# The first four down-score matmuls at the head of each score burst

## The chip, the cores and the metric

The kernel runs on one core of a Trainium2 chip. The metric is the device time of one execution in microseconds. Three runs of the kernel before gave 315.98, 316.63 and 320.5 us; the median is 316.63.

## The reference

An attention block with two branches feeds a two-matrix MoE expert. Shapes: batch B = 8, H = 8 heads, S = 576 positions, D = 64. Cut to what is computed:

```python
q_d, k_d, v_d = (mean over 4 neighbouring positions of q, k, v)   # 144 positions
out_up = repeat(sm_attn(q_d, k_d, v_d), 4, axis=2)                # "down" branch
mask = abs(pos[:, None] - pos[None, :]) < 4                       # "local" branch
scores = where(mask, q @ k.T / sqrt(D), -1e9)
out_local = softmax(scores) @ v
x = (out_up + out_local) as [B * S, H * D]                        # 4608 x 512
h = x @ w_in                                                      # 512 x 2048
out = (h * sigmoid(1.702 * h)) @ w_out                            # 2048 x 512
```

## The kernel before

The 4608 tokens go through the MoE in nine groups of 512 (loop `for g in range(n_groups)`). `mm1` multiplies by `w_in` (128x512 matmuls, L682) and applies the activation on ScalarE (L693); `mm2` multiplies by `w_out` (L746). The attention of batch g + 1 is woven into group g. The order on each engine is written by hand: `POS` and `POS_G` name the steps of `mm1` and `mm2` ahead of which a part of the attention is issued. The parts are, for each batch: the first score burst (`s_pe(0)`, four of the eight heads), its exponentials (`s_act(0)`), the second score burst with its exponentials (`s1`), two steps that multiply by v (`av`, L439 and L448), and the transposes (`tr`, L490). Each stands on TensorE as a short burst between long MoE matmuls. Batch 0 has its own functions (`scores`, `scores_d`) in the start-up part and runs before the loop, so `scores_mixed` is called for batches 1 to 7, twice each.

A score burst (`scores_mixed`) has two kinds of matmuls on small tiles of the array, each with a weight load of its own. A local score (`score`, L367) takes 32 rows of the array and 64 columns and streams 60 columns; there are 80, in groups of four over the four 32-row strips. A group of one `x` uses one 64-column half for even strips and the other half for odd ones, the next group the opposite halves. A down-score (`score_d`, L379) has the same tile size, streams 144 columns, and is issued in sets of four, one per strip; there are six sets (three chunks `kc` times two halves `a` of D), 24 matmuls. The locals write two PSUM buffers `sp`, the down-scores a third, `sd`; the three buffers `pa` serve all parts of the attention in turn.

What the burst reads: `kT` and `qT` come from VectorE transposes (L267); `kdT` and `qdT`, the sums over four positions, from GpSimd (`pool_qk`, L297 and L301), in batch 1's second burst from VectorE (L286). Its results are read by ScalarE: `exp_local` (L417) reads the two `sp` buffers, `exp_down` (L423) the `sd` buffer. The second burst of a batch writes the same three buffers, so it waits for these exponentials.

An instruction that waits for one semaphore does so itself. Where a weight load waits for two engines, a separate semaphore instruction stands ahead of it; the trace shows it on the weight loads' sequencer. In the kernel before, the first weight load of L379 in the second burst of batches 2 to 7 waits for ScalarE and GpSimd.

Of the kernel before, what the change touches and what calls it, by code (L numbers as in the profile page):

```python
# [19 lines left out]
def kernel(  # L20
# [51 lines left out]
    def ps_tile(n=None):  # L72
        if n is None:
            n = turn["a"] % 3
            turn["a"] += 1
        return PA[n]
# [286 lines left out]
    def score(b, qd, sp, i, a, par, r, barred=False):  # L363
        rows = slice(32 * r, 32 * r + 32)
        k0 = 114 * i + KSTART[par]
        q0 = 114 * i + QSTART[par]
        nc.tensor.matmul(  # L367
            sp[r // 2][64 * par : 64 * par + 64, r % 2, 60 * i : 60 * i + 60],
            lhsT=kT[b, qd][rows, k0 : k0 + 64, a],
            rhs=qT[b, qd][rows, q0 : q0 + 60, a],  # L370
            start=(a == 0 and not barred),
            stop=(a == 1 or barred),
            tile_position=(32 * r, 64 * par),
            skip_group_check=barred,
        )

    def score_d(b, qd, sd, kc, a, r):
        rows, j = slice(32 * r, 32 * r + 32), r % 2
        nc.tensor.matmul(  # L379
            sd[64 * j : 64 * j + 64, r // 2, SD * kc : SD * kc + SD],  # L380
            lhsT=kdT[qd][rows, 48 * kc : 48 * kc + 64, a],
            rhs=qdT[b, qd][rows, :, a],
            start=(a == 0), stop=(a == 1),
            tile_position=(32 * r, 64 * j),
        )
# [16 lines left out]

    def scores_mixed(b, qd):
        sp, sd = [ps_tile(), ps_tile()], ps_tile()
        for i in range(5):
            for a in range(2):
                if i >= 2:
                    for r in range(4):
                        score_d(b, qd, sd, i - 2, a, r)
                for x in (1, 0):  # L410
                    for r in range(4):
                        score(b, qd, sp, i, a, r % 2 if x == 0 else 1 - r % 2, r)
        return sp, sd
# [230 lines left out]
    def attention(b, slots=None):  # L644
        st = {}

        def s_pe(qd):
            st["s", qd], st["d", qd] = scores_mixed(b, qd)
# [232 lines left out]
    for g in range(n_groups):  # L881
        b = g + 1
# [74 lines left out]
```

## Time and profile before

| what | value |
|---|---|
| median of three runs | 316.63 us |
| profiled execution | 317.56 us |
| its span, first to last instruction | 315.8 us |
| granted TensorE clock | 0.998 |
| matmuls of L367, mean life of one | 1280, 198 ns |
| matmuls of L746 and L682 (into `pm`), mean life | 528 and 512, 380 and 379 ns |
| one mixed score burst, first matmul to next MoE matmul | 0.99 us |

Times are microseconds from the start of the span. In a timeline row the columns are start, length, engine, source line, operation, destination and sources, tile of the array, operand shape and count; several instructions of one kind are merged into one row, and its length runs to the end of the last. PE is TensorE's matmuls, PEld its weight loads. Matmuls overlap: the life of one is longer than the distance to the next. An end of a matmul is modelled, a start is recorded.

### The profile page before, as it was taken

What the parts mean: (1) busy time and instruction counts of PE and PEld (TensorE: products, weight loads), DVE (VectorE), ACT (ScalarE), POOL (GpSimd) and SP (SyncE); (2) the same over time, 40 slices, a digit from 0 to 9 for tenths busy, and PEclk for the clock granted to TensorE, in tenths of its full rate; (3) what the DMA queues carried; (4) which work ended last, traced back from release to release, by engine and by line L of the source; (5) the groups of instructions that cost most, each with busy time, mean ns of one, the idle gap of its engine ahead of it and who ended that gap; (6) DMA issues with size and microseconds to landing.
All of it is one profiled execution on the core that took longest, in us unless ns stands there. A gap on an engine that the chain in (4) does not pass through costs nothing.

```text
span 315.8 us, 10270 instructions
## 1 busy us (share of the span) xinstructions
PE 307.7 (97%) x4543; PEld 154.3 (49%) x4543; DVE 123.5 (39%) x247; ACT 190.2 (60%) x348; POOL 138.8 (44%) x170
## 2 busy tenths in 40 slices
PE   7989999999999999999999999999999999999995
PEld 3455455445544455455544554455445544444444
DVE  6763824720673057604760377027801640000000
ACT  5445882767657685668566856584767576316611
POOL 8863782179339920794079505960393000000000
PEclk9999999999999999999999999999999999999999
DMA  7999999999959913995299519971920110020011
GB/s 119 122 187 210 187 86 205 190 196 261 181 162 224 202 47 98 188 204 113 87 203 206 112 56 206 208 136 39 173 46 11 58 71 2 15 85 33 2 66 66
DMA packets 64075, 39.97 MB, mean 127 GB/s; under 512 B 44064, under 2 KB 55456, under 8 KB 64032
## 3 DMA queue, kind: packets, MB, share of 16 engines
q1 hardware_dynamic: 44496, 24.32, 36.0%
q0 software_dynamic: 19392, 14.95, 33.5%
q8 instruction: 35, 0.57, 0.8%
q14 instruction: 8, 0.07, 0.1%
q10 hardware_dynamic: 144, 0.07, 0.1%
HBM read 44.83 MB, written 9.44 MB: 172 GB/s over the span
## 4 chain that ended last, share of the span: by engine, by line
PE 91%; DMA 4%; ACT 1%; POOL 1%; issue 1%; DVE 0%; POOLq 0%; DVEq 0%; ACTq 0%
PE pm L746 36%; PE pm L682 35%; PE pa L682 4%; PE pa L367 2%; PE pa L439 2%; DMA qb<-in_q_dram 2%; PE pa L490 2%; PE pa L379 2%; PE pa L746 2%; PE pa L448 2%; DMA vb<-in_v_dram 1%; PE pm L761 1%; ACT od L610 1%; PE pm L640 0%; POOL vb L221 0%
## 5 line engine op out<-in xcount | busy, mean ns | idle before, releaser
L746 PE MATMUL pm<-w_out_bf,gT 128*128 128x512 bf16 x528 | 120.3, 380 | 0.0
L682 PE MATMUL pm<-xT,w_in_bf 128*128 128x512 bf16 x512 | 119.2, 379 | 0.5 <-ACT xT L603 0.3
L693 ACT ACTIVATE gT<-pm 128x512 bf16<-128x512 f32 x128 | 76.3, 598 | 43.7 <-PE pm L682 43.7
L682 PEld LDWEIGHTS <-w_in_bf 128*128 128x128 bf16 x576 | 55.7, 98 | 66.9 <-issue 1.1
L746 PEld LDWEIGHTS <-gT 128*128 128x128 bf16 x560 | 52.3, 98 | 60.7 <-issue 0.5
L431 DVE TENSOR_TENSOR es<-es,mask 128x600 bf16<-128x600 bf16 x28 | 19.0, 694 | 97.0 <-ACT es L417 96.3
L297 POOL TENSOR_TENSOR pq<-kT 128x576 f32<-128x576 bf16 x13 | 15.1, 1165 | 60.8 <-DVE kT L267 60.8
L731 ACT ACTIVATE osb<-pm 128x512 f32<-128x512 f32 (+2 forms) x35 | 20.4, 587 | 25.8 <-PE pm L746 23.0
L476 DVE TENSOR_TENSOR y<-pa,rc 128x896 bf16<-128x896 f32 x28 | 30.6, 1092 | 1.0
L480 ACT COPY y<-y 64x64 bf16<-64x64 bf16 x28 | 6.7, 241 | 31.3 <-DVE y L476 31.3
L417 ACT ACTIVATE es<-pa 128x600 bf16<-128x600 f32 x32 | 19.7, 668 | 8.7 <-PE pa L367 8.6
L313 POOL TENSOR_TENSOR v<-v 112x512 f32<-112x512 f32 x18 | 23.0, 1279 | 0.0
L307 POOL CAST vb<-vf 128x2560 bf16<-128x2560 f32 x6 | 13.9, 2318 | 19.8 <-DMA out_dram<-osb 6.3
L267 DVE STREAM_TRANSPOSE kT<-kb 128x576 f32<-128x576 f32 x16 | 19.9, 1246 | 5.8 <-DMA kb<-in_k_dram 5.6
L733 DVE TENSOR_SCALAR osb<-pm 128x128 f32<-128x128 f32 x1 | 0.3, 292 | 55.2 <-ACT osb L731 55.2
L632 DVE TENSOR_TENSOR xT<-pa,od 128x456 bf16<-128x456 bf16 (+2 forms) x84 | 16.6, 255 | 12.3 <-ACT od L610 12.1
L267 DVE STREAM_TRANSPOSE qT<-qb 128x576 f32<-128x576 f32 x16 | 19.9, 1243 | 0.8 <-DMA qb<-in_q_dram 0.4
L682 PE MATMUL pa<-xT,w_in_bf 128*128 128x512 bf16 x64 | 20.0, 379 | 0.0
L610 ACT COPY od<-pa 128x256 bf16<-128x256 bf16 (+1 forms) x56 | 18.3, 410 | 1.1 <-PE pa L490 0.4
L367 PEld LDWEIGHTS <-kT 32*64 32x64 bf16 x1280 | 14.2, 104 | 6.9 <-issue 4.1
L221 POOL DMA_DIRECT2D vb<-in_v_dram x20 | 13.7, 703 | 8.6 <-DMA w_in_bf<-in_moe_w_in_dram 3.6
L367 PE MATMUL pa<-qT,kT 32*64 32x60 bf16 x1280 | 16.5, 198 | 0.5 <-DVE qT L267 0.5
(90 smaller groups left out, 275.9 us busy)
## 6 DMA issues: line engine op xcount, KB each, us to landing
out_dram<-osb SPq DMA_DIRECT2D x35, 256.0 KB, 2.4
vf<-in_v_dram SPq DMA_DIRECT2D x60, 128.0 KB, 6.8
v<-in_v_dram SPq DMA_DIRECT2D x36, 192.0 KB, 5.4
kb<-in_k_dram POOLq DMA_DIRECT2D x16, 288.0 KB, 7.7
qb<-in_q_dram POOLq DMA_DIRECT2D x16, 288.0 KB, 8.9
w_in_bf<-in_moe_w_in_dram POOLq DMA_DIRECT2D x4, 512.0 KB, 9.2
w_out_bf<-in_moe_w_out_dram POOLq DMA_DIRECT2D x4, 512.0 KB, 12.5
vb<-in_v_dram POOLq DMA_DIRECT2D x20, 64.0 KB, 5.9
```

The source lines that it names most:

```text
L267: nc.vector.transpose(out=t32.rearrange("p (i c) -> p c i", c=18), in_=store[b, qd].bitcast(FP32).rearrange("p (c d) -> p c d", c=18),)
L313: eng.tensor_tensor(out=t1[0:112], in0=x[:, :, 0:2, :], in1=x[:, :, 2:4, :], op=ALU.add)
L367: nc.tensor.matmul(sp[r // 2][64 * par : 64 * par + 64, r % 2, 60 * i : 60 * i + 60], lhsT=kT[b, qd][rows, k0 : k0 + 64, a], rhs=qT[b, qd] ...
L417: nc.scalar.activation(out=es[2 * qd + u][:, :, 0:300], in_=sp[u][:, :, 0:300], func=AF.Exp, scale=inv_sqrt_d,)
L431: nc.vector.tensor_tensor(out=ev, in0=ev, in1=mask, op=ALU.mult)
L476: nc.vector.tensor_tensor(out=y.rearrange("p (x c) d -> p x c d", x=2), in0=ov[:, :, :, 0:D], in1=rc.to_broadcast([128, 2, 7, D]), op=ALU. ...
L610: nc.scalar.copy(out=od[:, 4 * t0 : 4 * (t0 + n)].rearrange("p (t f) -> p t f", f=4), in_=x[:, xx, c0 : c0 + n, None].to_broadcast([128, n ...
L632: nc.vector.tensor_tensor(out=sub(xT[hp], t0 + at, *dims), in0=sub(x, col, *from_x), in1=sub(od, at, *dims), op=ALU.add,)
L682: nc.tensor.matmul(acc, lhsT=w_in_bf[:, dmc, ffc * 128 : (ffc + 1) * 128], rhs=xT[dmc][:, g * TG : g * TG + TG], start=(dmc == 0), stop=(d ...
L693: nc.scalar.activation(out=gT[:, ffc, :], in_=acc, func=AF.Silu, scale=GELU_SCALE)
L731: eng.activation(out=osb, in_=ap, func=AF.Copy, scale=1.0 / GELU_SCALE)
L746: nc.tensor.matmul(ops[t], lhsT=gT[:, ffc, t * 128 : (t + 1) * 128], rhs=w_out_bf[:, ffc, :], start=(ffc == 0), stop=(ffc == n_ffc - 1),)
```

## The change

`scores_mixed` keeps a list of the six sets of down-scores. The first set is issued ahead of all locals. The others follow as before, one set ahead of each group of eight locals from chunk i = 2 on, until the list is empty. So the order in a burst was 32 locals, then six times (4 down-scores, 8 locals); it becomes 4 down-scores, 32 locals, five times (4 down-scores, 8 locals), 8 locals. On the other engines the order of instructions is the same in both kernels.

```diff
     def scores_mixed(b, qd):
         sp, sd = [ps_tile(), ps_tile()], ps_tile()
+        down = [(kc, a) for kc in range(3) for a in range(2)]
+
+        def next_down():
+            kc, a = down.pop(0)
+            for r in range(4):
+                score_d(b, qd, sd, kc, a, r)
+
+        next_down()
         for i in range(5):
             for a in range(2):
-                if i >= 2:
-                    for r in range(4):
-                        score_d(b, qd, sd, i - 2, a, r)
+                if i >= 2 and down:
+                    next_down()
                 for x in (1, 0):
                     for r in range(4):
                         score(b, qd, sp, i, a, r % 2 if x == 0 else 1 - r % 2, r)
```

## The prediction

> **What bounds the kernel.** I read the busy table, the chain of waits, then the timeline of TensorE inside one score burst and around its start. The first two, from the page:
>
> ```profile
> PE 307.7 (97%) x4543; PEld 154.3 (49%) x4543; DVE 123.5 (39%) x247; ACT 190.2 (60%) x348; POOL 138.8 (44%) x170
> ...
> PE 91%; DMA 4%; ACT 1%; POOL 1%; issue 1%; DVE 0%; POOLq 0%; DVEq 0%; ACTq 0%
> ```
>
> TensorE is the bound and has almost no idle time, so whatever a score burst gains or loses on TensorE reaches the end. The granted clock is 0.998. There are 14 mixed bursts (batches 1 to 7, two each); batch 0 uses other functions and is untouched. The timeline of TensorE around one of them (start, length, line, tile, count):
>
> ```profile
> 103.86 0.81 PE L682 MATMUL pm<-xT,w_in_bf 128*128 128x512 bf16 x3
> 104.60 0.33 PE L367 MATMUL pa<-qT,kT 32*64 32x60 bf16 x32
> 104.84 0.27 PE L379 MATMUL pa<-qdT,kdT 32*64 32x144 bf16 x4
> 104.87 0.27 PE L367 MATMUL pa<-qT,kT 32*64 32x60 bf16 x8
> ...
> 105.40 0.26 PE L367 MATMUL pa<-qT,kT 32*64 32x60 bf16 x6
> 105.59 0.60 PE L682 MATMUL pm<-xT,w_in_bf 128*128 128x512 bf16 x2
> ```
>
> The burst takes 0.99 us, in two regimes. The 32 leading locals are all in within 0.14 us (the row ends at 104.93, a local lives about 0.19, so the last began at 104.74). Then nothing starts for 0.10 us. From 104.84 on the other 72 matmuls come at an even pace: each round of 4 down-scores and 8 locals takes 0.10 us, 8.3 ns per matmul with its weight load. What makes the gap? Not the down-scores or their semaphores. The start-up burst of batch 0 has 80 locals in a row, nothing between; here the same timeline cut at 8.50 and at 8.54:
>
> ```profile
> 8.30 0.34 PE L367 MATMUL pa<-qT,kT 32*64 32x60 bf16 x32
> ```
>
> ```profile
> 8.30 0.42 PE L367 MATMUL pa<-qT,kT 32*64 32x60 bf16 x33
> ```
>
> There too number 33 starts about 0.24 us after number 1. 32 matmuls with their 32 weight loads are 64 instructions. My reading: 64 instructions can be waiting or in flight, a place comes free when an instruction completes, and number 33 must wait until number 1 (0.21 us from start to end) is through, plus 0.026. The burst at 12.04 supports it: its number 1 lived 0.18 us and its number 33 came 0.21 us after the start. After that the stream of instructions, at 8.3 ns a pair, sets the pace. So the last matmul starts at 0.238 + 71 x 0.0083 = 0.829 us after the first by that pace; measured 0.86. The 0.03 between is the tail: the last locals use the array tiles of the four down-scores just before them, and wait for those.
>
> **The change, part by part.** Nothing is added or removed: 80 locals and 24 down-scores per burst, all weight loads, DMAs and other queues stay. Four down-scores move from place 33 to place 1; the five other sets each move one step earlier; the last 8 locals have none ahead of them.
>
> *The array's own time at the head.* A down-score first on an idle array lives longer than a local. From the start-up burst of 24 down-scores alone, cut at its first:
>
> ```profile
> 17.36 0.25 PE L379 MATMUL pa<-qdT,kdT 32*64 32x144 bf16 x1
> ```
>
> So number 33 starts at 0.25 + 0.026 = 0.276 us instead of 0.238: +0.04 per burst. The four down-scores and 28 locals must be in by then: four down-scores hold their tiles some 0.09 us (in that burst the next ones on the same tiles begin 0.09 later), and the remaining locals go at 32 per 0.14 us, so about 0.09 + 24 x 0.0044 = 0.20 us. Covered, with 0.07 to spare.
>
> *The tail.* The 0.03 goes. Net +0.01 per burst, x14 = +0.1 us. Bounds: if number 33 stays at 0.238, -0.03 x 14 = -0.4; if nothing of the tail goes, +0.04 x 14 = +0.6. I take +0.1, since both terms have a row.
>
> *The waits, first burst of a batch.* The first down-score needs kdT and qdT from GpSimd now at once, 0.24 us earlier. Its sums (the pooling line L301) end 2.7 us before the burst in batch 1 and 6 us or more in the others (65.58 against 71.77, 98.28 against 104.60): no wait; for the second bursts the sums end over 4 us ahead (75.43 against 79.69). Its PSUM buffer was last read in the batch before. Cost nothing; with that cover gone at most 0.24 a burst.
>
> *The waits, second burst.* Here the down-score buffer is the one that the exponential of the first burst (L423) reads, and the wait for it moves from place 33 to place 1. Burst and exponential, two of them:
>
> ```profile
> 111.41 0.90 ACT L423 ACTIVATE ed<-pa 128x864 bf16<-128x864 f32 x1
> ...
> 112.38 0.33 PE L367 MATMUL pa<-qT,kT 32*64 32x60 bf16 x32
> ```
>
> ```profile
> 42.56 0.90 ACT L423 ACTIVATE ed<-pa 128x864 bf16<-128x864 f32 x1
> ...
> 43.33 0.33 PE L367 MATMUL pa<-qT,kT 32*64 32x60 bf16 x32
> ...
> 43.56 0.27 PE L379 MATMUL pa<-qdT,kdT 32*64 32x144 bf16 x4
> ```
>
> At 112.38 the exponential ended 0.07 us earlier, and so in all six batches from 2 on; in batch 1 it ends 0.13 after the burst began. Before, the 0.24 us of locals covered this exactly. From ScalarE's end to a waiting matmul I have one row: the exponential at 44.45 (0.67 long) ends at 45.12, and the matmul that reuses its buffer starts at 45.17: 0.05. In the six the weight load waits for two engines at once, and the trace shows a separate step for that:
>
> ```profile
> L379 PEldq EVENT_SEMAPHORE  x6: 51/51/51, 79.8 to 243.3; - x6
> ```
>
> It takes 0.05, and the load follows 0.025 later. So start = end of exponential + 0.05 + 0.05 + 0.025, which is 0.06 us later than now: 6 x 0.06 = 0.36 (from 0.01 each if that step overlaps the wait, 0.07 in all). Batch 1 waits plainly: 0.13 + 0.05 = 0.19. That the 64 places are then not filled ahead costs little: at 8.3 ns a pair number 33 is there after 0.27 us, when it is due anyway. Behind the wait stand the rest of the burst and all later MoE matmuls, so it is on the path. ScalarE's exponentials after the burst and VectorE's masks move with TensorE.
>
> *Sum.* 0.1 + 0.36 + 0.19 = +0.65 us. The profiled execution (317.56, span 315.8 and 1.8 around it) would come to 318.2; it lies 0.9 above the median of the runs shown, 316.63, so I forecast 317.3.
>
> **Rivals.**
> A, *only the tail counts*: number 33 stays at 0.238 and the semaphore steps overlap: -0.4 + 0.07 + 0.19 = -0.15, 316.5. For it: the life of a down-score has one such row. Against: number 33 followed number 1's end in both start-up bursts. Chance 0.25.
>
> B, *the gap was the wait*: the pause before the first down-score is caused by its semaphores and goes when these are met during the MoE matmuls. Each burst then runs at 8.3 ns a pair from the start, 0.238 us less: 14 x -0.238 + 0.55 = -2.8, 313.8. Against: the start-up burst has the gap without down-scores. Chance 0.07.
>
> C, *the slow side*: the second bursts start cold. TensorE's stream stands at the wait, the 64 places are empty, and after the release they take another 0.24 us to fill, as a stretch of 0.24 is seen whenever they ran dry. Place: the head of seven bursts; price 7 x 0.24 = 1.7 more: 319.0. It decides if the first down-score starts over 0.25 us after the exponential's end. Against: the plain wait above released in 0.05. Chance 0.15.
>
> D, *loads held behind down-scores*: the locals after the first four use the same 32-row strips, and if their weight loads can't pass the running down-scores, 28 locals begin at 0.25, number 32 at 0.37 and number 33 behind it: +0.1 per burst, 14 x 0.1 + 0.55 = +1.9, 318.6. Against: at 104.84 the eight locals on the same strips start 0.03 after four down-scores that live 0.27. The Trainium skill, "TensorE: Matmul & The Clock Gate", Part 3 under "The mechanism", says that a weight load overlaps running matmuls only when its row group differs. By that rule this rival holds; the rows at 104.84 speak against it, for tiles in another column half. Chance 0.06.
>
> **How the numbers follow.** The forecast has 0.44, A 0.25, B 0.07, C 0.15, D 0.06; 0.03 is for what I haven't seen. Two of the three runs lie within 0.65 of each other, the third at 320.5, so I allow 0.8 to either side: low 315.4 is A's lower bound (-0.4 alone, 316.2) less 0.8; high 319.1 takes in C and, with 0.8, the forecast's own upper bound (0.6 + 0.36 + 0.19, 317.8). Left out are B and part of C, D and the unseen, some 0.2. Two per cent is 6.3 us, about what a measurement of this kernel can tell from no change. Over 14 bursts that would be 0.45 us of each burst's 0.99. No case comes near: faster 0.02, within 0.95, slower 0.03 (the unseen).
>
> **What would show it.** In the changed trace: in first bursts the gap between matmuls 32 and 33 is still there, number 33 at about 0.276 after number 1, burst length (first matmul to next MoE matmul) 0.99 to 1.00. In second bursts the first matmul is 0.37 us after the MoE matmul before it instead of 0.31, in batch 1 0.50, and the separate semaphore step stands ahead of the burst. Bursts of 0.75 us mean B; 0.6 us between exponential's end and burst mean C; locals 0.25 us behind the first down-scores mean D.

## The result, and the profile after

The changed kernel takes 319.33 us (median of 22 runs, 318.16 to 322.82) against 316.54 for the kernel before (22 runs, 315.87 to 320.5). The ratio is 1.0085, interval 1.0065 to 1.0104: slower by 2.7 us (2.1 to 3.3), and within 2%. The forecast was 317.3 with a range up to 319.1: the direction is right, the size is not.

The profiled execution after took 320.5 us, with a span of 318.7, 2.9 longer than before. Its page (busy time of the engines; the queue that carries instructions; the chain that ended last):

```profile
PE 308.3 (97%) x4543; PEld 155.1 (49%) x4543; DVE 123.6 (39%) x247; ACT 190.4 (60%) x348; POOL 139.0 (44%) x170
...
q8 instruction: 35, 0.57, 0.8%
...
PE 82%; DMA 6%; SPq 4%; ACT 2%; DVE 2%; issue 2%; POOL 2%; POOLq 0%; DVEq 0%; ACTq 0%
```

The busy time of TensorE hardly moves (307.7 to 308.3), so 2.3 of the 2.9 us are time in which TensorE does nothing. (The chain's larger shares of DMA and SyncE come from one pause, shown below, that the profile puts down to a GpSimd cast: the chain goes back from it through that cast's transfers.) I looked for the lost time in the bursts, as TensorE's timeline shows them. First a first burst, the one of batch 3 that the prediction showed:

```profile
103.83 0.81 PE L689 MATMUL pm<-xT,w_in_bf 128*128 128x512 bf16 x3
104.57 0.26 PE L379 MATMUL pa<-qdT,kdT 32*64 32x144 bf16 x4
104.59 0.49 PE L367 MATMUL pa<-qT,kT 32*64 32x60 bf16 x32
104.88 0.26 PE L379 MATMUL pa<-qdT,kdT 32*64 32x144 bf16 x2
...
105.34 0.32 PE L367 MATMUL pa<-qT,kT 32*64 32x60 bf16 x14
105.59 0.60 PE L689 MATMUL pm<-xT,w_in_bf 128*128 128x512 bf16 x2
```

From its first matmul (104.57) to the next MoE matmul (105.59) the burst takes 1.02 us; before it took 0.99. Read to the nanosecond, the stretch from the last MoE matmul to the next is 1.324 us in six of the seven first bursts (1.322 to 1.326) against 1.294 before: +0.03. (Batch 2's has some 0.15 more in both kernels, 1.484 and 1.438.) The locals begin 0.02 after the first down-scores.

Now the second burst of batch 3: the timeline of ScalarE, the weight loads (PEld) and the matmuls around its start, and the row of the separate semaphore steps of line 379:

```profile
111.42 0.90 ACT L430 ACTIVATE ed<-pa 128x864 bf16<-128x864 f32 x1
...
111.64 0.81 PE L753 MATMUL pm<-w_out_bf,gT 128*128 128x512 bf16 x3
...
112.43 0.14 PEld L379 LDWEIGHTS <-kdT 32*64 32x64 bf16 x4 [0.47 <-issue]
112.46 0.26 PE L379 MATMUL pa<-qdT,kdT 32*64 32x144 bf16 x4
```

```profile
L379 PEldq EVENT_SEMAPHORE  x7: 51/51/51, 16.4 to 245.3; - x7
```

The exponential ends at 112.31, the semaphore step starts 0.037 later and lasts 0.051, the matmul starts at 112.46. From the last MoE matmul to the burst (the entry) there are 0.384 us in all six of batches 2 to 7 instead of 0.309, and the whole stretch is some 1.40 instead of 1.293 (1.395 to 1.400; batch 4's has a pause of 0.1 in it besides, 1.494). In batch 1, with its later exponential, the entry is 0.465 and the stretch 1.476 instead of 1.291.

So the bursts explain 7 x 0.03 + 0.185 + 6 x 0.10 = 1.0 us. The rest lies elsewhere, in bursts that the change does not touch. TensorE in the first step by v of batch 4, after and then before:

```profile
148.86 0.34 PE L446 MATMUL pa<-vb,es 64*64 64x65 bf16 x17
149.89 0.21 PE L455 MATMUL pa<-vd,ed 48*64 48x65 bf16 x1 [0.68 <-POOL vb L307]
...
150.59 0.82 PE L753 MATMUL pm<-w_out_bf,gT 128*128 128x512 bf16 x3
```

```profile
148.41 0.34 PE L439 MATMUL pa<-vb,es 64*64 64x65 bf16 x17
148.56 0.19 PE L448 MATMUL pa<-vd,ed 48*64 48x65 bf16 x1
...
149.25 1.04 PE L746 MATMUL pm<-w_out_bf,gT 128*128 128x512 bf16 x4
```

Matmul 18 comes 1.03 us after matmul 1 instead of 0.15. The timeline puts 0.68 of that down to a GpSimd cast, but that cast ended at 149.24. The weight load ahead of the matmul, which waits for no semaphore, is as late:

```profile
149.88 0.10 PEld L455 LDWEIGHTS <-ed 48*64 48x64 bf16 x1 [0.79 <-issue]
```

The profiled execution of the changed kernel has eight such pauses (the length given is the distance between the starts of the two matmuls around it): 0.23 at 51.76 (batch 1), 0.43 at 84.42 and 0.97 at 88.71 (batch 2), 0.20 at 116.82, 0.11 at 145.50, 0.87 at 149.01, 0.50 at 153.12 (batches 3 and 4), 0.92 at 249.01 (batch 7): 4.2 us. Before there were two, 0.45 at 53.12 and 0.25 at 246.75. All lie at the same kind of place in TensorE's instruction list. Counting its weight loads, matmuls and sequencer steps through the trace from 0, the first instruction behind a pause, a weight load or a matmul, is number 193 above a multiple of 256 in all ten. The page's q8 row says what a place of that kind is: 35 packets with 0.57 MB are 35 blocks of 16 KB, and the 9100 instructions that the trace has of TensorE make 35.5 blocks of 256. I call the place between two blocks a border. The Trainium skill, "Runtime: NRT & Kernel Launch", "Instruction fetch mechanics", says the same (blocks of 256 instructions, fetched by the sequencer over a queue of its own while the block before runs) and calls a crossing "mostly hidden". In this execution it was hidden at most of the 35 borders and cost up to 0.97 us at eight.

The sum closes: 1.0 from the bursts and 3.5 from more pauses, less 1.6 because the first mixed burst of this execution began at 37.84 instead of 39.43, gives the 2.9 of the two spans. One execution is one draw of the pauses, though; the median says 2.7, so 1.7 (1.1 to 2.3) is to be explained besides the bursts.

### The profile page after: what moved, and what is told of

Same layout as the page of the kernel before. It is cut to its first block, busy times and chain, and to the rows that moved or that the text cites. A ratio compares the mean times of both kernels' runs of the same rounds, so it can differ in the third digit from the quotient of the medians.

```text
span 318.7 us, 10270 instructions
## 1 busy us (share of the span) xinstructions
PE 308.3 (97%) x4543; PEld 155.1 (49%) x4543; DVE 123.6 (39%) x247; ACT 190.4 (60%) x348; POOL 139.0 (44%) x170
## 4 chain that ended last, share of the span: by engine, by line
PE 82%; DMA 6%; SPq 4%; ACT 2%; DVE 2%; issue 2%; POOL 2%; POOLq 0%; DVEq 0%; ACTq 0%
PE pm L753 32%; PE pm L689 31%; PE pa L689 4%; SPq L210 3%; PE pa L446 2%; DMA qb<-in_q_dram 2%; PE pa L367 2%; DMA vf<-in_v_dram 2%; PE pa L379 2%; PE pa L753 2%; PE pa L497 2%; PE pa L455 2%; DMA v<-in_v_dram 1%; PE pm L768 1%; PE pm L647 1%
## 5 line engine op out<-in xcount | busy, mean ns | idle before, releaser
L297 POOL TENSOR_TENSOR pq<-qT 128x576 f32<-128x576 bf16 x14 | 16.1, 1147 | 0.1
```

Of the source, the lines that this page charges most:

```text
L297: nc.gpsimd.tensor_tensor(out=t1, in0=sv[:, :, 0:2, :], in1=sv[:, :, 2:4, :], op=ALU.add)
```

## The experiments

**The theory.** The sequencer is the part of the engine that fetches instructions and hands them over. A plain wait for one semaphore stays with its instruction, and the sequencer goes on handing over the ones behind it, up to 64 ahead: among MoE matmuls at 0.216 us each, 32 matmuls or, as an estimate, at most 7 us. The separate semaphore step is executed by the sequencer itself. While it waits for the exponential, the sequencer passes nothing behind it. With the step at the head of a second burst, the sequencer comes to the next block border only with the burst instead of microseconds ahead; the transfer of the following block starts late, and the next dense burst reaches that block before it is there. In batch 4 the border lies 7 instructions behind the step. The rival: only the bursts' own lengthening counts, and the pauses come and go with the execution.

Where the expectations use letters, H is this theory and R the rival. The first four kernels ran in turn on one chip, so did the next four, and the last three, each time with runs of the kernel before among them.

**First bursts alone.**

```diff
-        next_down()
+        if qd == 0:
+            next_down()
```

> The change in the first bursts of each batch alone (7 of 14); the second bursts keep the old order. Theory H (the sequencer is held at the separate semaphore step that now heads the second bursts): first bursts have no such step, so only the +0.03 us per burst that the changed trace shows in the array and stream (1.324 against 1.294 us from MoE matmul to MoE matmul), 7 x 0.03 = +0.2 us against the kernel before, and no more pauses at every 256th instruction than before (three, 0.8 us). Rival R (the order itself or the array costs it, wherever it stands): half of the +2.7, so +1.3.

316.82 us, ratio 1.0011 (0.9985 to 1.0036): no difference that can be told from none. The first bursts take 1.323 to 1.326 in four batches, +0.03, and up to 0.14 more in the three others; the second ones begin as before (0.309 entry). But its profiled execution, 318.24 us and so 1.4 above its median, has a pause of 0.41 in batch 1 and two in batch 2 that no theory had listed (0.97 and this one of 1.05):

```profile
84.30 0.21 PE L447 MATMUL pa<-vb,es 64*64 64x65 bf16 x1
85.35 0.32 PE L447 MATMUL pa<-vb,es 64*64 64x65 bf16 x16 [0.84 <-issue]
```

**Second bursts alone.**

```diff
-        next_down()
+        if qd == 1:
+            next_down()
```

> The change in the second bursts alone. H: nearly all of it, +2.5 us against the kernel before: six bursts start 0.07 late, batch 1's 0.16 late, +0.03 each for the order, in all 0.9, and the rest in pauses at every 256th TensorE instruction in the bursts after, 1.5 us or more beyond the three of before. R: half, +1.3.

318.1 us, ratio 1.005 (1.0025 to 1.0074): +1.6 us. The bursts account for 0.8. Pauses: 0.22 in batch 2, 0.17 in batch 3, 0.10, 1.14 and 0.50 in batch 4. The time goes with the second bursts, but it is less than the theory's 2.5 and, taken alone, nearer to the rival's 1.3. Against the rival stands that the first bursts cost 0.3 (-0.5 to 1.1) and not 1.3.

**The whole change, with each instruction waiting for one engine.** The order of the two sums on GpSimd is turned round for the second half of the heads. Then the weight load waits for GpSimd alone and its matmul for ScalarE alone, and no separate step is made.

```diff
-        for name, src in (("k", kT), ("q", qT)):
+        pairs = (("k", kT), ("q", qT))
+        for name, src in pairs[::-1] if qd else pairs:
```

> The whole change, and GpSimd sums q before k for the second four heads. By that the first weight load of the second bursts waits for GpSimd alone and its matmul for ScalarE alone: two plain waits at the same place, no separate semaphore step; the same work in the same order on TensorE. H: the sequencer runs ahead as before; the six bursts start on time (0.31 us after the MoE matmul; ScalarE's end + 0.05 is 0.01 before that), pauses as before; left are 14 x 0.03 and batch 1's 0.16: +0.6 us. R: +2.7 as in the changed kernel, or +2.3 if the late start alone goes.

317.41 us, ratio 1.0007 (0.9972 to 1.0042). The six steps are gone, one in the start-up part is left:

```profile
L380 PEldq EVENT_SEMAPHORE  x1: 51/51/51, 17.6 to 17.6; - x1
```

The second bursts begin on time (entry 0.309) and batch 4's step by v has no pause:

```profile
147.66 0.34 PE L447 MATMUL pa<-vb,es 64*64 64x65 bf16 x17
147.81 0.19 PE L456 MATMUL pa<-vd,ed 48*64 48x65 bf16 x1
```

Two pauses are left, 0.19 at 214.41 and 0.41 at 246.42. The first four down-scores still stand at the head of every burst; without the step the loss is gone.

**The kernel before, with the step alone.** One single down-score of the first set, and with it the wait, goes to the head of the second bursts of batches 2 to 7; the rest stays in the old order.

```diff
+        one = qd == 1 and b > 1
+        if one:
+            score_d(b, qd, sd, 0, 0, 0)
...
-                    for r in range(4):
+                    for r in range(one and i + a == 2, 4):
```

> The kernel before, with a single down-score (chunk 0, half 0, strip 0) of the second bursts of batches 2 to 7 moved to place 1, its three companions staying at place 33. It takes the separate semaphore step with it. H: the step holds the sequencer as in the changed kernel: bursts 0.07 late, +0.03 each, six bursts 0.6 us, and pauses at every 256th instruction: together +2 us, near the change in second bursts alone. R (it is the order of the four sets, or the array): a fourth of a set moved in six bursts, +0.2 us or nothing.

318.3 us, ratio 1.0057 (1.0028 to 1.0087): +1.8 us. The bursts account for 6 x 0.09 = 0.5. The rival had 0.2 or nothing. Pauses again in batches 2 to 4 (0.30; 0.19; 0.17, 0.63 and 0.22), the longest of them here:

```profile
147.65 0.34 PE L442 MATMUL pa<-vb,es 64*64 64x65 bf16 x17
148.43 0.21 PE L451 MATMUL pa<-vd,ed 48*64 48x65 bf16 x1 [0.45 <-issue]
```

**The control: the kernel before with GpSimd's order turned.** The same edit as in the third kernel, without the change.

> Control: the kernel before with only the GpSimd order of the one-wait kernel (q before k for the second four heads). Its separate semaphore step stood at place 33 of the second bursts and goes. H: at place 33 it cost nothing (matmul 33 starts 0.238 us after the first with and without it), so 0 (within 0.5 us of the kernel before), and the one-wait kernel's gain over the changed kernel isn't GpSimd's. R': the GpSimd order helps by itself: -1 us or more.

316.94 us, ratio 1.0003 (0.9974 to 1.0032). The order on GpSimd does nothing by itself.

**One group of locals first.** The third kernel, with four locals ahead of the first four down-scores.

```diff
-        next_down()
         for i in range(5):
...
                     for r in range(4):
                         score(b, qd, sp, i, a, r % 2 if x == 0 else 1 - r % 2, r)
+                    if i + a == 0 and x == 0:
+                        next_down()
```

> The one-wait kernel with one group of four locals ahead of the first four down-scores. Window theory (64 instructions in flight; matmul 33 waits for the end of matmul 1): matmul 1 is a local again, 0.212 us of life, matmul 33 at 0.238 instead of 0.275 after the first, a burst 1.295 instead of 1.325 us from MoE matmul to MoE matmul: 14 x 0.03 = 0.4 us less than the one-wait kernel. Rival (the down-scores' own occupancy of the tiles delays the rest): matmul 33 stays at 0.275.

316.92 us, ratio 1.0003 (0.9964 to 1.0043). This tests what the prediction says of number 33:

```profile
103.34 0.22 PE L368 MATMUL pa<-qT,kT 32*64 32x60 bf16 x4
103.35 0.26 PE L380 MATMUL pa<-qdT,kdT 32*64 32x144 bf16 x4
103.39 0.42 PE L368 MATMUL pa<-qT,kT 32*64 32x60 bf16 x28
...
103.63 0.27 PE L380 MATMUL pa<-qdT,kdT 32*64 32x144 bf16 x4
```

Number 1 is now a local, whose life is 0.21 and not 0.25. Number 33 is the last but three in the row of 28 locals; it starts 0.237 to 0.240 after number 1 instead of 0.273 to 0.280 in the third kernel, and number 37 follows at 103.63. The stretch shrinks to 1.303 to 1.308, not to the 1.295 that I had expected. (This holds for 13 bursts; batch 1's second one waits for its exponential.) The 0.02 us a burst, 0.3 in all, can't be seen in the times.

**The second bursts two steps later.** The changed kernel with the second burst two MoE steps later, so that the exponential is over well before it.

```diff
-    POS = [13, 16, 35, 45, 54, 65]
+    POS = [13, 16, 37, 45, 54, 65]
...
-        2: [13, 16, 35, 48, 57, 67],
+        2: [13, 16, 37, 48, 57, 67],
-        5: [13, 16, 35, 48, 57, 67],
+        5: [13, 16, 37, 48, 57, 67],
-        6: [13, 16, 35, 45, 57, 67],
+        6: [13, 16, 37, 45, 57, 67],
```

> The changed kernel with the second burst two MoE matmuls later (35 becomes 37 in the tables of steps; batch 1 keeps its place). The exponential is then over 0.36 us before the burst, but the sequencer stands at the separate semaphore step until the same time, 6 instructions ahead of the block border in batch 4. H: the six bursts start 0.31 us after the MoE matmul instead of 0.38, 0.45 us less than the changed kernel, and the pauses of batches 3, 4 and 7 at every 256th instruction stay, since the next block is asked for when the sequencer passes the border: about +2.2 against before. Rival (the pauses come from the late start): they go, +0.6.

318.43 us, ratio 1.007 (1.0052 to 1.0088): +2.2 us by the ratio. The second bursts now begin on time (entry 0.308 to 0.310, stretch 1.324 to 1.329, batch 1's too), and the pauses stay: 0.30 in batch 3, 0.69 and 0.22 in batch 4, 0.40 in batch 7. The first of batch 4's:

```profile
147.85 0.34 PE L446 MATMUL pa<-vb,es 64*64 64x65 bf16 x17
148.69 0.21 PE L455 MATMUL pa<-vd,ed 48*64 48x65 bf16 x1 [0.50 <-issue]
```

This parts the two costs of the step: the late start of the burst is gone, and the pauses are there without it. The step is still executed only when the exponential has ended, now 0.46 us ahead of the burst instead of 0.11.

**The borders moved.** In the changed kernel a warm-up of TensorE in the start-up part is replaced by 64 tiny matmuls with weight loads, 120 instructions more. Only warm-up work is changed.

```diff
-    warm(2, z=wf)
+    t = pm_tile()
+    for _ in range(64):
+        nc.tensor.matmul(
+            t[0:64, 0:8], lhsT=wz[:, 0:64], rhs=wz[:, 0:8], start=True, stop=True
+        )
```

> The changed kernel with two float32 warm-up matmuls of the start-up replaced by 64 tiny matmuls with their loads; TensorE's later instructions keep their order and stand 120 instructions further on. H: the pauses stand at block borders of 256 instructions, so they move by 120: none at the places of the changed kernel in batch 4's steps by v and batch 2's, and new ones at other instructions, all 256 (or multiples) apart: in the list of the changed kernel at numbers 45 (+-4) modulo 256 instead of 165; most likely in the first step by v of batch 2, where a border stands 31 instructions behind the held step. Time between +1 and +3.5. Rival (pauses belong to the work at those places): they stay at the same matmuls.

326.03 us, ratio 1.0268 (1.021 to 1.0326). As a price it can't be used, and the expected time was missed: the granted clock was 0.984 to 0.989 in all six runs, and the start-up part is 4.7 us longer (first mixed burst at 42.54 against 37.84). What it shows is where the pauses go. They stand at 193 above a multiple of 256 again, counted in its own trace, which are other instructions of the kernel: none in batch 4, whose border is now some 140 instructions behind the step, and new ones. The largest, 2.67 us, is in batch 1. In batch 2, where a border now lies some 30 instructions behind the step, there are three, one in the second burst (0.16) and one in each step by v (1.47 and 0.77), as batch 4 had them in the changed kernel. The first step by v:

```profile
89.21 0.25 PE L455 MATMUL pa<-vd,ed 48*64 48x65 bf16 x7
90.74 0.25 PE L455 MATMUL pa<-vd,ed 48*64 48x65 bf16 x6 [1.28 <-issue]
```

So the pauses belong to the borders and not to the matmuls, and the group of three went, as expected, to the batch where a border follows the step closely.

**Three second looks**, a single run each: the changed kernel, the one with first bursts alone, and the kernel before.

> The changed kernel once more, for a second profile. H: the pauses of batches 3, 4 and 7 at block borders (in batch 4: both steps by v, 0.87 and 0.50 us in the first profile) come again within 0.4 us each, since the held step causes them; those of batch 2 (0.43 and 0.97), where no border stands close behind the held step, may be absent. If all come and go freely, the held step isn't their cause.

319.97 us. Batch 4's pauses are there again (0.14, 0.60, 0.50), and batch 3's (0.13 instead of 0.20). Batch 2 has one of 0.23 instead of 0.43 and 0.97, batch 6 one of 0.23, and batch 7 one of 0.15 at 253.14 instead of 0.92 at 249.01. The expectation held for batches 3 and 4 and failed for batch 7. Two longer stops in batch 1 (TensorE 0.95 and 0.73 behind its MoE pace) lie at no border; the trace shows them waiting for the DMA of `w_out`.

> The change in the first bursts alone once more. Its first profile had pauses of 1.03 and 0.94 us in batch 2 and was one of its slower executions (318.2 against a median of 316.8). H: these depend on when a block's transfer starts among the other transfers, not on the order of the burst; at a time near 316.3 they are absent. Rival (the order in first bursts causes them): they come again.

317.67 us. The pauses of batch 2 are gone:

```profile
85.16 0.34 PE L447 MATMUL pa<-vb,es 64*64 64x65 bf16 x17
85.31 0.19 PE L456 MATMUL pa<-vd,ed 48*64 48x65 bf16 x1
```

So the pauses of batch 2 come and go with the execution, as the rival has it, and need no step at the head. Whether the step makes them more frequent is open: four of the five profiles with it have some in batch 2, and one of the seven without.

> The kernel before once more, for a second profile. H: no pause in batch 4 at block borders, and the block that batch 4's first step by v needs is asked for before the second burst begins, as in its first profile (0.3 us ahead). Batch 2's pauses may appear in a slow execution.

315.6 us, no pause in batch 4.

**The transfers side by side.** The transfer of the block that the first step by v of batch 4 runs into (packet times on q8), against the second burst of batch 4 that comes some 3 us ahead of that step; the last columns are the matmul behind the border and the pause ahead of it:

```
kernel                          second burst  transfer        begins     matmul   pause
                                begins        from - to       after it   behind
no step at the head
  before                        145.16        144.87-146.21   -0.29      148.57   -
  before, second look           143.36        142.18-143.47   -1.18      146.77   -
  before, GpSimd turned         148.17        147.12-148.31   -1.05      151.57   -
  first bursts alone            145.74        144.57-145.89   -1.17      149.14   -
  first alone, second look      144.61        143.75-145.09   -0.86      148.02   -
  whole change, one wait        144.38        143.31-144.55   -1.07      147.82   -
  one group of locals first     143.85        142.91-144.20   -0.94      147.27   -
step at the head
  changed                       145.49        147.60-148.53   +2.11      149.89   0.87
  changed, second look          145.75        146.95-148.52   +1.20      149.90   0.60
  second bursts alone           144.25        146.50-147.45   +2.25      148.91   1.14
  one down-score ahead          144.26        145.48-147.00   +1.22      148.43   0.63
  two steps later               145.00        146.07-147.39   +1.07      148.69   0.69
```

Without the step the transfer begins 0.3 to 1.2 us before the burst, with it 1.1 to 2.3 us after, and 1.3 to 2.4 us after the step is executed. It takes 0.9 to 1.6 us, and where there is a pause the matmul behind the border runs 1.30 to 1.46 us after its end. There is no overlap between the two groups. (The kernel with shifted borders has no border here and is left out.)

Such a shift is seen in batch 4 alone. In batch 3 it is small (the transfers begin 0.8 to 2.0 us behind the border with the step and 0.9 to 1.1 without it), and in batches 5 to 7, where the border lies 44 to 190 instructions behind the step, the transfers begin 0.5 to 1.8 us behind the border with the step and 0.8 to 1.7 us without it. The pauses agree: those of batches 3 and 4 add up to 1.2 to 1.9 us in each of the five profiles with the step and to nothing in the seven without; those of the other batches are 0.2 to 2.6 us with it and 0 to 2.4 us without.

The times say the same. For each kernel, what its bursts explain (from its own profile, pauses left out) and what was measured, in us against the kernel before of the same call:

```
kernel                     step at the head   bursts   measured (interval)
changed                    yes                 1.0      2.7 ( 2.1 to 3.3)
second bursts alone        yes                 0.8      1.6 ( 0.8 to 2.3)
one down-score ahead       yes                 0.5      1.8 ( 0.9 to 2.8)
two steps later            yes                 0.4      2.2 ( 1.6 to 2.8)
first bursts alone         no                  0.2      0.3 (-0.5 to 1.1)
whole change, one wait     no                  0.6      0.2 (-0.9 to 1.3)
one group of locals first  no                  0.3      0.1 (-1.1 to 1.4)
GpSimd turned              no                  0.0      0.1 (-0.8 to 1.0)
```

By the middle values all four kernels with the step lose 0.8 to 1.8 us more than their bursts explain, about what the pauses of batches 3 and 4 are in their profiles, and the four without it at most 0.1; the intervals are wide, and that of second bursts alone reaches down to its bursts. None beats the kernel before.

**What stays open.** That the sequencer stands at the step, and so reaches the border late, is inferred: the trace shows when the step executes and when the transfers begin, not where the sequencer is in between. Nor does the table show a lead of several us: without the step the transfer begins at most 1.2 us ahead of the burst. (In the kernel with shifted borders the last two transfers begin 4.1 and 3.8 us ahead of their borders, among MoE matmuls.) And a transfer can be late without a step: in the first bursts of batches 2 to 6, in the twelve profiles of the table, it begins 2.6 to 4.3 us behind the border, and in batch 2's second burst 1.3 to 3.7, with and without the step. There the next border mostly comes late enough. Why these transfers are late was not tried; that other transfers hold them up is only a guess.

## Why the prediction was wrong in size

**The step that failed** is the sentence on the second bursts' wait: "That the 64 places are then not filled ahead costs little: at 8.3 ns a pair number 33 is there after 0.27 us, when it is due anyway." For the burst itself it is right: number 33 comes after 0.247 us, and once begun, the second bursts are 0.028 longer than before, as much as the first ones, which don't wait. But I asked only what the places not filled cost inside the burst. What they cost is behind it: in batch 4 the transfer of the block that the first step by v runs into begins 1.1 to 2.3 us after the burst instead of before it, and TensorE stops at the border. By the medians that is 1.7 of the 2.7 us, and nothing in my sum stood for it. That the lost lead of the sequencer is what delays the transfer is my inference. The profile of before had shown the thing twice, as two pauses with no semaphore to explain them, and a queue named "instruction" in its list; I hadn't read either.

The other steps, one by one:

- *Number 33 at 0.276 us.* Right in the first bursts: 0.274 to 0.276, and 0.237 to 0.240 with a local in the first place. In most second bursts it is 0.247, where number 1 lives 0.22. These are as much longer than before as the first ones all the same, so the time of number 33 doesn't set the length of a burst by itself, as the sum had it.
- *The tail's 0.03 goes.* Wrong: it moves. The last local now waits for nothing, but the distance from it to the next MoE matmul grew from 0.125 to 0.141, so that only about 0.007 went. Head and tail make +0.03 a burst and not +0.01, or 0.4 us over 14 bursts and not 0.1; why the next MoE matmul keeps its distance is open. This is within the bound that I had written (nothing of the tail goes, +0.6).
- *First bursts wait for nothing.* Right: entry 0.309 in all seven.
- *The semaphore step, +0.06 in six bursts.* Mechanism right; +0.075 measured. I had 0.125 from the exponential's end to the matmul and it is 0.14: 0.037 to the step, 0.051 of the step, the rest to the load and matmul.
- *Batch 1, +0.19.* Measured +0.156.
- *The sum of the bursts*: 0.65 forecast, 14 x 0.03 + 6 x 0.075 + 0.156 = 1.0 measured.

The rivals. A (only the tail counts) is out: the head's cost came and the tail's gain did not. B (the gap was the wait) is out: the first bursts' down-scores wait for nothing and the burst is 1.02 long, not 0.75. C (second bursts start cold) has the time nearest to the measured one, 319.0, and is still wrong as I priced it: from the exponential's end to the matmul there are 0.14 us and not over 0.25, and no burst pays 0.24. If my inference holds, it had the right circumstance, that the stream stands at the wait and the places are empty, and the wrong place for the bill. D (loads held behind down-scores) is out: in the second burst of batch 3 the locals' weight loads on the same strips begin at 112.47, 0.01 after down-scores that live until 112.72. The rule of the Trainium skill, "TensorE: Matmul & The Clock Gate", Part 3, that a load overlaps running matmuls only when its row group differs does not hold here for tiles in another column half.

The chances for "within 2%" came out; the range ended 0.2 below the median because it held no case in which the cost falls outside the bursts.

## What to carry to other kernels

A wait for two engines on one instruction can cost more than its 0.05 us: where a block border lay close behind it (7 instructions in batch 4), the following block came late, and TensorE stood for 0.6 to 1.1 us at its border. Ordering the producers so that each instruction waits for one engine took this away here (0.2 us slower than before, -0.9 to 1.3, instead of 2.7), and the order of the producers cost nothing by itself. Where TensorE pauses in a dense burst and no semaphore explains it, look at the instruction's number in the program and at the instruction queue's transfers before blaming the work around it.

## What the hardware showed that I had not expected

- TensorE's instructions come in blocks of 256, one transfer of 0.9 to 1.8 us each in the twelve profiles of the table. Where TensorE paused at a border, the first instruction behind it came 1.3 to 1.6 us after the end of its transfer; only the pauses of 0.10 to 0.17 us inside batch 4's second burst stand at a block that had been there for longer. In these profiles, from the first mixed burst on, a transfer begins between 2.4 us before and 4.3 us after the instruction at the border before it runs, so at most the block in use and the next are there. A score burst starts its 208 instructions in 0.87 us, less than one transfer takes. The Trainium skill, "Runtime: NRT & Kernel Launch", "Instruction fetch mechanics", gives TensorE 128 KiB, which would be eight blocks, and adds that there are only two lines; the transfers here agree with two.
- Number 33 followed the (modelled) end of number 1 by 0.026 us whether number 1 was a local (0.238) or a down-score (0.276). This agrees with 64 places of which one comes free only when an instruction completes.
- The end of a burst is not set by its last matmul alone: with one group of locals first, the last local starts 0.856 us after the first matmul instead of 0.861 before, and the next MoE matmul comes after 0.996 instead of 0.986.
